# Attention denominators from a ones column of V, spread by a VectorE shuffle, in a one-core block kernel with a written-out order

## The chip, the core and the metric

The kernel runs on one core of a Trainium2 chip. A core has TensorE (PE, which multiplies matrices; PEld is its loading of weights), VectorE (DVE), ScalarE (ACT), GpSimd (POOL), SyncE (SP, which here only starts DMAs) and 16 DMA engines. The metric is the time of one execution in device microseconds. The kernel before took 169.4 us, the median of three runs (169.27, 169.4 and 171.14 us).

## The reference, cut to what matters

One block of a transformer on 2048 tokens of width 448, conditioned by a vector `c`:

```python
sa, ca, ga, sb, cb, gb = (silu(c) @ w_mod) in six rows
h = layernorm(x) * (1 + ca) + sa
q, k, v = h @ wqkv                                  # 16 heads of width 28
idx = pos[:, None] - 2 * arange(8)[None, :]         # 8 keys per query, 2 apart
logits = einsum('bhsd,bhswd->bhsw', q, k[idx]) * 28 ** -0.5
o = einsum('bhsw,bhswd->bhsd', softmax(logits, masked where idx < 0), v[idx])
x = x + ga * (o @ wo)
h = layernorm(x) * (1 + cb) + sb
x = x + gb * (gelu(layernorm(h) @ w1 + b1) @ w2 + b2)
```

## The kernel before

**Tiles.** Keys lie 2 tokens apart, so even and odd tokens never meet; they are two halves (`NS = 2`) of 1024 positions. A *token tile* p (0 to 7) is 128 positions of both halves. Attention goes in nine *batches* i (0 to 8) of 114 query positions, each as two windows (`j`) of 57 queries over 64 keys. The MLP goes in four *MLP tiles* t of two token tiles.

**Stages.** `front_ln` normalizes a token tile on DVE into a `zy` buffer (`stats`, `rstd`, `normalize`, `tail`), turns it on its side (by PE for tiles 0 and 1, by an SP transpose DMA `zT<-zy` for the others) and `affine` makes `hT` of it. `front_qk` makes q and k of tiles 0 and 1; `natural_qk` does so for tiles 2 to 7 (PE into `pq`, a copy into `zy`, transpose DMAs into `qT` and `kT`). `attention(i)` makes V of its windows (`pv`, copied to a `vb` buffer with 32 columns per head, of which 28 are V and 4 are padding), the logits (`lt`), their exponentials (`et`, ACT), the band mask (DVE multiplies `et` by `mask`), then on PE the denominators (`pd`) and the weighted values (`po`). The denominators' reciprocal is made on ACT as exp(-ln) in `den`, and the DVE product `omul` writes `po` times `den` into `qT`, over the queries that are no longer needed.

In `pd`, 8 matmuls per batch multiply a matrix of ones by `et`, so that all 32 rows of a head hold the sum of its weights; for the first window of batch 0 the first seven keys do not exist, and `ones_k` has zeros there:

```python
nc.tensor.matmul(pd.t[HP * r:HP * r + HP, j, 0:2 * SBE], lhsT=ones_k[rows, int(i == j == 0), :],
                 rhs=et.t[rows, r].rearrange("p m c -> p (m c)"), ...)
```

`out_proj(p)` (matmuls `wo{p}` into `pw`) needs the `omul` of the batches that cover tile p: batches 0 and 1 for tile 0, 1 and 2 for tile 1, 2 and 3 for tile 2, 3 and 4 for tile 3. It adds the residual on DVE (named `x1`), makes the second and third layernorm, and ends in a transpose DMA `yT<-zy`. `mlp(t)` multiplies by `w1` (tiles `p`, from `yT`), applies gelu on ACT, multiplies by `w2` and stores. ACT has to load another table between exponentials and gelu, so the work is cut into `PHASES`: batches 0 to 4 and MLP tile 0; batches 5 and 6 and MLP tile 1; batches 7 and 8 and MLP tiles 2 and 3.

**What sets the order.** Every step is a numbered task with the tasks it needs. Nothing is scheduled on the chip: `ORDER` lists the task numbers in the order in which they are written into the engines' queues, each queue runs strictly in that order, and `SLOTS` says which buffer of its kind each tile gets. An entry `84:A` gives the task to ACT (A), DVE (D) or POOL (P) instead of its usual engine; `55+12@55` writes 12 *fillers* ahead of task 55, which are matmuls on zeros into a PSUM tile that is free at that moment. PSUM has four places of two banks for `pq`, `pv`, `lt`, `pd`, `po`, `pw` and the MLP's tiles. ACT's and POOL's table and mask set-up, all DMA starts of SP and the constant fills of DVE are tasks too.

Of the kernel before, what the change touches and what calls it, by code (L numbers as in the profile page):

```python
# [15 lines left out]
KT, KS = 4, 64  # L16
# [33 lines left out]
]  # L50
ORDER = """
3 14 17 0 1 15 5 9 10 18 11 16 13 19 20 2 6 24 21 73 55+12@55 26 12 71 25 56 72 74 57 75 22 58 77 23 59 62 60 27 61 76
4 32 67 66 78 68+11@68 108 63 28 110 64 30 84:A 89:P 69 79 65 31 70 88:P 109 111 80 83 112:P 34 81 87:A 85 29 93:P
90:A 101+9@101 114 113 36 82 94+3@94 91 95 115:D 92:A 102 86 103 116 144 96 120:A 97 99 135 104 106 117:A 98 142 118:A
105 145 119:A 143 133 146 100 121 136 134 148 137 126 107 147 7 149:D 138 127 150 122 139 124 129 198 190 123 140 191
200 141 199 128 269 125 271 236 270 130 207 40 209 33 201 241 210 38 237 208 272 238 273 37 185 242 152 202 35 154 151
153:A 8 278 187 239 203 159 211 204 188 205:D 212 206 155 279 213 186 243 240 214:A 160 156 192 215 307 157 189 275
161 274 158 280 171 308 281 282 193 162 172 244 245 284 195 283 163 217 173 285 246 276:D 219 39 218 167 216 277 247
447 164 196 248 225 286 168 224 165 169:D 174 312 42 309 313 228 166 310 314 220 170 226 311 290 221 289 229 222 288
315 194 287 230 558 232 197 317 176 560 233 318 175 316 177 223 249 319 234 49 227 320 250 231 251 559 321 235 345 253  # L60
342 346 373:R 254 252 324 46 255 343 322 44 257 48 340 561 323 325 256 41 326 258 374 51 482 54 378 344 375 52 379 299
347 47 259 376 43 328 292 327 300 341 260 348 291 329 301 261 330 295 293 262 263 380 350 264 294 131 296 132 304 333
297 303 377 45 351 334 331 381 265 349 332 305 266 335 382 352 267:A 483 383 268 337 336 384 448 338:D 339 385 353 53
# [89 lines left out]
def kernel(  # L153
# [143 lines left out]
    dconst(0.45, consts, ["vpad", "ones"])  # L297
# [664 lines left out]
```

## Time and profile before

| | before |
|---|---|
| median of three runs | 169.4 us |
| the profiled execution | 170.37 us, of which the span of the core is 168.6 us |
| busy: PE, DVE, ACT, POOL | 95%, 67%, 60%, 25% of the span |
| matmul instructions | 2126 |
| DMA | 18.78 MB, nearly all in the first 70 us |
| granted PE clock | full in every slice |

The span runs from the core's first instruction to its last; a profiled execution is one of many, and this one took 0.97 us more than the median of the three timed runs. The trace gives for each group of instructions the busy time, the mean length of one and the idle time of its engine just before it, with what ended that idle time. Instructions of one engine overlap at their ends, so what one more instruction costs is the distance between two starts in the timeline, which is a little less than its length.

### The profile page before, as it was taken

To read this page: it belongs to the slowest core of one execution; us is meant where nothing else is said; L and a number is where in the kernel's file an instruction comes from. 1 tells how busy PE (TensorE), PEld (TensorE's weight loads), DVE (VectorE), ACT (ScalarE), POOL (GpSimd) and SP (SyncE) were. 2 spreads that over 40 slices of the span, in tenths; PEclk is the share of its full clock that TensorE was granted. 3 is DMA by queue.
4 is the path that set the end of the run, shared out by engine and by line. 5 is a ranking of instruction groups with operands and counts; after the bars stand their busy time and mean duration, and the time that the engine had idled before them with its cause. 6 is when DMAs were issued, how large, how long until landed. Compare 5 with 4: busy or idle time off the path is not lost.

```text
span 168.6 us, 4965 instructions
## 1 busy us (share of the span) xinstructions
PE 160.9 (95%) x2126; PEld 84.0 (50%) x2126; DVE 113.2 (67%) x277; ACT 101.3 (60%) x139; POOL 42.0 (25%) x69
## 2 busy tenths in 40 slices
PE   7999969987999999999999999999999999999992
PEld 4778535444554544435565443555544455344562
DVE  7869898758899969897837869465596940400112
ACT  3378888949379946869557167986318440099000
POOL 3235251002030400319300033850003156008100
PEclk9999999999999999999999999999999999999999
DMA  5999989699999799300150000028020006110002
GB/s 158 323 336 291 167 253 172 129 158 255 188 227 287 211 160 201 100 0 0 25 106 2 4 0 2 4 49 188 4 95 14 0 4 120 46 67 0 0 27 82
DMA packets 35573, 18.78 MB, mean 111 GB/s; under 512 B 28507, under 2 KB 34592, under 8 KB 35552
## 3 DMA queue, kind: packets, MB, share of 16 engines
q1 hardware_dynamic: 35548, 18.47, 47.6%
q8 instruction: 16, 0.26, 0.6%
q14 instruction: 5, 0.04, 0.1%
q10 hardware_dynamic: 4, 0.00, 0.0%
HBM read 9.81 MB, written 1.84 MB: 69 GB/s over the span
## 4 chain that ended last, share of the span: by engine, by line
PE 77%; DMA 13%; DVE 4%; issue 2%; POOL 2%; SPq 1%; ACT 1%; POOLq 0%; DVEq 0%
PE p L882 26%; PE p L547 22%; PE pw L802 7%; DMA zT<-zy 7%; PE pq L547 5%; PE p L553 4%; DMA x_all<-in_A_x_dram 4%; PE pv L547 3%; PE po L770 3%; DMA wm_st<-in_w_mod_dram 3%; PE lt L737 2%; DVE hT L501 2%; PE pv L705 2%; PE pd L759 1%; DVE stt L455 1%
## 5 line engine op out<-in xcount | busy, mean ns | idle before, releaser
L863 ACT ACTIVATE hm<-p,b_col 128x512 bf16<-128x512 f32 x56 | 33.6, 695 | 30.6 <-PE p L553 26.1
L882 PE MATMUL p<-w_s,hm 128*128 128x448 bf16 (+1 forms) x238 | 44.5, 342 | 0.0
L547 PE MATMUL p<-yT,w_s 128*128 128x512 bf16 x168 | 38.1, 380 | 0.0
L468 POOL TENSOR_TENSOR rs_all<-mvs,neg_half 128x2 f32<-128x2 f32 x23 | 16.4, 719 | 75.1 <-DVE mvs L457 75.1
L882 PEld LDWEIGHTS <-hm 128*128 128x128 bf16 x238 | 22.6, 98 | 18.9 <-issue 0.6
L547 PEld LDWEIGHTS <-w_s 128*128 128x128 bf16 x168 | 15.8, 98 | 21.0 <-issue 3.2
L888 DVE TENSOR_TENSOR x_all<-p,x1p 128x896 bf16<-128x896 f32 (+2 forms) x10 | 8.8, 899 | 23.7 <-PE p L882 23.7
L744 ACT ACTIVATE et<-lt 128x928 bf16<-128x928 f32 x18 | 16.1, 940 | 6.7 <-PE lt L737 6.6
L455 DVE BATCH_NORM_STATS2 stt<-x_all 128x6 f32<-128x448 bf16 x32 | 18.6, 610 | 1.6 <-DMA x_all<-in_A_x_dram 1.4
L547 PE MATMUL pq<-wqk_st,hT 128*128 128x448 bf16 x72 | 15.0, 353 | 1.8 <-DVE hT L501 1.5
L840 POOL TENSOR_TENSOR x1p<-x_all,gbb_bc 128x448 f32<-128x448 bf16 x16 | 16.5, 1060 | 0.0
L787 DVE TENSOR_TENSOR qT<-po,den 128x912 bf16<-128x912 f32 x9 | 10.0, 1106 | 7.1 <-ACT den L781 6.7
L802 PE MATMUL pw<-wo_s,qT 128*128 128x448 bf16 x64 | 13.1, 353 | 0.0
L750 DVE TENSOR_TENSOR et<-et,mask 128x928 bf16<-128x928 bf16 x18 | 11.0, 640 | 2.2 <-ACT et L744 2.1
L627 ACT CAST zy<-pq 128x896 bf16<-128x896 f32 x11 | 9.7, 911 | 2.7 <-issue 2.0
L809 DVE TENSOR_TENSOR x_all<-pw,x_all 128x896 bf16<-128x896 f32 x8 | 8.7, 1088 | 3.9 <-PE pw L802 3.9
L779 ACT ACTIVATE den<-pd 128x928 f32<-128x928 f32 x9 | 8.5, 952 | 4.7 <-PE pd L759 4.7
L818 DVE TENSOR_TENSOR h<-h,mod_bc 128x896 bf16<-128x896 bf16 x16 | 10.4, 655 | 0.2
L547 PEld LDWEIGHTS <-hT 128*128 128x128 bf16 x72 | 6.5, 98 | 8.1 <-DVE hT L501 2.0
L455 DVE BATCH_NORM_STATS2 stt<-h 128x6 f32<-128x448 bf16 x16 | 9.5, 611 | 0.1
L781 ACT ACTIVATE den<-den,den_bias 128x928 f32<-128x928 f32 x9 | 9.4, 1068 | 0.2
L802 PEld LDWEIGHTS <-qT 128*128 128x128 bf16 x64 | 6.0, 98 | 6.0 <-issue 0.4
(114 smaller groups left out, 177.3 us busy)
## 6 DMA issues: line engine op xcount, KB each, us to landing
w_s<-in_B_w_dram SPq DMA_DIRECT2D x7, 224.0 KB, 3.3
out_dram<-x_all SPq DMA_DIRECT2D x7, 224.0 KB, 2.0
x_all<-in_A_x_dram SPq DMA_DIRECT2D x3, 448.0 KB, 6.5
wmod<-in_w_mod_dram SPq DMA_DIRECT2D x3, 448.0 KB
w_s<-in_B_w_dram SPq DMA_DIRECT2D x3, 448.0 KB, 4.8
wqk_st<-in_A_wqkv_dram SPq DMA_DIRECT2D x3, 225.0 KB, 4.3
wm_st<-in_w_mod_dram SPq DMA_DIRECT2D x1, 672.0 KB, 4.6
x_all<-in_A_x_dram SPq DMA_DIRECT2D x2, 224.0 KB
```

Source lines behind the costliest of these rows:

```text
L455: add("DVE", 0.53, lambda: nc.vector.bn_stats(out=stt[:, w, b, 0:6], in_=src()), reads=reads, bufs=bufs, after=early if w == b == 0 else ( ...
L468: ways = {"POOL": (0.55 + 0.17 * n, lambda: nc.gpsimd.tensor_tensor(out=r, in0=v, in1=neg_half[:, 0:n], op=ALU.pow))}
L547: nc.tensor.matmul(out(), lhsT=lhs(kt, slice(0, 128)), rhs=rhs(kt, slice(0, 128)), start=first and kt == 0, stop=not first and kt == KT - 2)
L627: add("ACT", 0.80, lambda to=to, src=src: nc.scalar.copy(out=to(), in_=src()), bufs=[pq, st], reads=["zpad"], writes=[(st, 0)], name="evac ...
L744: exps.append(add("ACT", 0.83, lambda half=half, lt=lt: nc.scalar.activation(out=et.t[:, 2 * half:2 * half + 2].rearrange("p r m c -> p r ...
L750: nc.vector.tensor_tensor(out=ev, in0=ev, in1=mask[:], op=ALU.mult)
L787: nc.vector.tensor_tensor(out=qT[:, :, LEAD + q00:LEAD + q00 + 2 * WQ], in0=po.t[:, :, 0:NS * 4 * WQ].rearrange("p j (m c) -> p m j c", c=WQ),
L802: nc.tensor.matmul(pw.t[:, s, 0:D], lhsT=qT[:, KT * s + ft, LEAD + 128 * p:LEAD + 128 * p + 128], rhs=wo_s[:, ft, :], start=(ft == 0), sto ...
L818: add("DVE", 0.55, lambda vec=vec, op=op: nc.vector.tensor_tensor(out=h2.t[:], in0=h2.t[:], in1=vec.unsqueeze(1).to_broadcast([128, NS, D] ...
L840: add("POOL", 1.0, lambda n=n: nc.gpsimd.tensor_tensor(out=x1p.t[:, n, :], in0=xn(p, n), in1=gbb2_bc[:], op=ALU.add), reads=[f"x{p}", "gbb ...
L863: gelus.append(add("ACT", 0.585, lambda f=f, a=a, p1=p1s[g]: nc.scalar.activation(out=hm.t[:, f].rearrange("p n c -> p (n c)"), in_=p1.t[: ...
L882: nc.tensor.matmul(p2.t[:, n, 0:c1 - c0], lhsT=hm.t[:, f, n, q * 128:(q + 1) * 128], rhs=w2_s[:, f, c0:c1], start=(f == parts[0][0]), stop ...
```

## The change

The denominators no longer have matmuls of their own. The 29th column of each head in `vb`, padding before, is filled with ones, so that row 28 of each head's 32 rows in `po` holds the sum of the weights. A new DVE instruction, `stream_shuffle`, copies that row to all 32 rows of its head, from `po` in PSUM into `den` in SBUF, as fp32. `Ln` on ACT then works in place on `den` (912 elements per row instead of 928, from SBUF instead of PSUM), followed by the same `Exp` and `omul`. For batch 0 the ones of the first seven keys are set to zero ahead of `po` and set back behind it. `pd` and its PSUM place are gone.

Beside this the reciprocal square root of tile 0's layernorm is split into two tasks, one for each half; a wait between two groups of `front_qk` is relaxed; eight PSUM places without work (`idle`) are added as targets for fillers; and `SLOTS` and `ORDER` are new as a whole (of them the diff shows the first and the last line of `ORDER`).

```diff
@@ SLOTS, ORDER: all lines
-3 14 17 0 1 15 5 9 10 18 11 16 13 19 20 2 6 24 21 73 55+12@55 26 12 71 25 56 72 74 57 75 22 58 77 23 59 62 60 27 61 76
+3 17 14 0 1 15 11 13 7 18 16 19 5 12 6 20 59+6@59 4 10 2 24 8 25 81 21 9 63+7@63 55 82 22 84:P 64 65 23 79 27 66 67 80
...
-680 691 688 689 694 693 701 683 692 682 684 695 685 702 697 703 704 709 698 696 710 699 705 711 700 706 712 707 708
+694 699 720 709 707 721 712 722 710 713 711 723 716 714 717 715 718 719 57+13@57 61+3@61
@@ consts
         for vb in vbufs:
-            nc.vector.memset(vb[:, :, :, DH:HP], 0.0)
-        nc.vector.memset(ones_k[:], 1.0)
-        nc.vector.memset(ones_k[0:WIN - 1, 1, :], 0.0)
+            nc.vector.memset(vb[:, :, :, DH:DH + 1], 1.0)
+            nc.vector.memset(vb[:, :, :, DH + 1:HP], 0.0)
@@ behind c_cols
+    for i in range(8):
+        idle = psum("idle")
+        add("PE", 0.0, lambda: None, reads=["warm_w"], bufs=[idle], fills=[idle], instr=0, name=f"fl{i}")
@@ front_ln
-            rstd(0, 2 * p, 2, on_act)
+            for b, m in ((2 * p, 1), (2 * p + 1, 1)) if p == 0 else ((2 * p, 2),):
+                rstd(0, b, m, on_act)
@@ front_qk
-    after=last_qk[-2:] if small and k else (),
+    after=last_qk[-1 if u[0] == 0 else -2:] if small and k else (),
@@ attention
+        ones = lambda value: nc.vector.memset(vb.t[0:WIN - 1, :, :, DH:DH + 1], value)
+        if i == 0:
+            add("DVE", 0.06, lambda: ones(0.0), reads=["vpad"], bufs=[vb], fills=[vb], name="ones")
...
-        add("PE", 0.25, dmm, reads=[(et, 0), (et, 1), "ones"], bufs=[et, pd], fills=[pd], mode="64x32", instr=16, name=f"pd{i}")
...
+        if i == 0:
+            add("DVE", 0.06, lambda: ones(1.0), bufs=[vb], needs=[P.tasks[-1]], name="ones")
-        den = sb("den", [128, 2, 4 * NS, WE], FP32, "den")
-        add("ACT", 0.87, lambda: nc.scalar.activation(out=flat(), in_=pd.t[:, :, 0:2 * SBE], func=ACT.Ln, scale=DEN_SCALE), ...
+        den = sb("den", [128, 2, 4 * NS, WQ], FP32, "den")
+        add("DVE", 1.0, lambda: nc.vector.stream_shuffle(out=den.t[:].rearrange("p j m c -> p j (m c)"), in_=po.t[:, :, 0:NS * 4 * WQ], mask=[DH] * HP),
+            bufs=[po, den], fills=[den], name="spread_den")
+        add("ACT", 0.87, lambda: nc.scalar.activation(out=den.t[:], in_=den.t[:], func=ACT.Ln, scale=DEN_SCALE), ...
```

What the new order does to the queues is seen at three places. The first is SP's queue of DMA starts right at the program's beginning, behind the loads of tile 0 and of the modulation weights (`x_all` is the input, `wqk_st` and `wqr_st` are the weights of q and k). Before:

```order
L338 DMA x_all<-in_A_x_dram 128x896
L324 DMA wqk_st<-in_A_wqkv_dram 128x900
L328 DMA wqr_st<-in_A_wqkv_dram 64x900 x2
L324 DMA wqk_st<-in_A_wqkv_dram 128x900 x2
L338 DMA x_all<-in_A_x_dram 128x2x896 x2
```

and in the change:

```order
L337 DMA x_all<-in_A_x_dram 128x896
L327 DMA wqr_st<-in_A_wqkv_dram 64x900
L323 DMA wqk_st<-in_A_wqkv_dram 128x900 x3
L337 DMA x_all<-in_A_x_dram 128x2x896
L327 DMA wqr_st<-in_A_wqkv_dram 64x900
```

One of the two `wqr_st` loads has moved behind the load of token tiles 2 and 3 (the first `128x2x896`).

The second place is DVE's queue from the first `omul` (`qT<-po,den`) to the first `x1` (`x_all<-pw,x_all`), in the middle of the first phase. Before:

```order
L688 COPY hw<-hT 128x1024
L787 TENSOR_TENSOR qT<-po,den 128x8x114
L628 CAST zy_98<-pq 128x32x28
L750 TENSOR_TENSOR et<-et,mask 128x928 x2
L501 TENSOR_SCALAR hT<-zT,mod_col 128x2x256 x4
L688 COPY hw<-hT 128x1024
L787 TENSOR_TENSOR qT<-po,den 128x8x114
L652 TENSOR_TENSOR wo_s<-wo_s,mod_bc 128x896 x2
L787 TENSOR_TENSOR qT<-po,den 128x8x114
L809 TENSOR_TENSOR x_all<-pw,x_all 128x896
```

and in the change, from the shuffle of batch 0 on:

```order
L778 STREAM_SHUFFLE den<-po 128x912
L504 TENSOR_SCALAR hT<-zT,mod_col 128x2x256 x2
L757 TENSOR_TENSOR et<-et,mask 128x928 x2
L480 TENSOR_SCALAR zy_98<-x_all,mvs,rs_all 128x448
L788 TENSOR_TENSOR qT<-po,den 128x8x114
L778 STREAM_SHUFFLE den<-po 128x912
L656 TENSOR_TENSOR wo_s<-wo_s,mod_bc 128x896 x2
L504 TENSOR_SCALAR hT<-zT,mod_col 128x2x256
L788 TENSOR_TENSOR qT<-po,den 128x8x114
L504 TENSOR_SCALAR hT<-zT,mod_col 128x2x256
L810 TENSOR_TENSOR x_all<-pw,x_all 128x896
```

Each `omul` has a shuffle ahead of it now; the window copies `hw<-hT` have left DVE's queue (one is on ACT, three are on POOL), and so has a part of the `hT` steps (to ACT).

The third place is DVE's queue where the third layernorms of token tiles 0 and 1 end (`zy<-h`), which their transposes wait for. Before:

```order
L477 TENSOR_SCALAR zy_99<-h_1206,mvs,rs_all 128x448
L787 TENSOR_TENSOR qT<-po,den 128x8x114
L477 TENSOR_SCALAR zy_96<-h_1320,mvs,rs_all 128x448 x2
L490 COPY zy_96<-zy_96 128x2x64
L787 TENSOR_TENSOR qT<-po,den 128x8x114
L809 TENSOR_TENSOR x_all<-pw,x_all 128x896
```

and in the change:

```order
L778 STREAM_SHUFFLE den<-po 128x912
L757 TENSOR_TENSOR et<-et,mask 128x928
L819 TENSOR_TENSOR h_1267<-h_1267,mod_bc 128x896
L480 TENSOR_SCALAR zy_98<-h_1203,mvs,rs_all 128x448
L458 BN_STATS stt<-h_1267 128x6 x2
L460 BN_AGGR mvs<-stt 128x2
L480 TENSOR_SCALAR zy_98<-h_1203,mvs,rs_all 128x448
L674 CAST b_col<-pb_1428 128x14
L460 BN_AGGR mvs<-stt 128x2
L778 STREAM_SHUFFLE den<-po 128x912
L480 TENSOR_SCALAR zy_99<-h_1267,mvs,rs_all 128x448 x2
L788 TENSOR_TENSOR qT<-po,den 128x8x114 x2
```

The shuffles of batches 3 and 4 stand ahead of these layernorms now, both `omul` behind them, and the small copy `zy<-zy` has gone to POOL.

More of the change, by code (lines that the diff above doesn't have):

```diff
@@ L56 @@
[L56 to L60, printed above, removed]
@@ L227 @@
     rs_all = cst.tile([128, 3, 2 * NP], FP32, name="rs_all")
-    ones_k = cst.tile([128, 2, HP], BF16, name="ones_k")
     den_bias = cst.tile([128, 1], FP32, name="den_bias")
@@ L598, in front_qk @@
                 last_qk.extend(summed([item(k, a) for a in range(2)], NS * n / 2400 + 0.0025,
-                                      ([] if first else [f"W{half}{k}" for k in range(KT - 1)] + [f"h{kt}_{p}" for kt in range(KT - 1) for p in u] + rk), [pqs[k]], [pqs[k]], after=last_qk[-2:] if small and k else (),
+                                      ([] if first else [f"W{half}{k}" for k in range(KT - 1)] + [f"h{kt}_{p}" for kt in range(KT - 1) for p in u] + rk), [pqs[k]], [pqs[k]], after=last_qk[-1 if u[0] == 0 else -2:] if small and k else (),
                                       name=f"qk{u[0]}_{half}" + "ab"[k], split=rk if first else None))
@@ L752, in attention @@
             add("DVE", 0.56, msk, port=True, bufs=[et], reads=["mask"], writes=[(et, half)], name="mask")
-        pd, po = psum("pd"), psum("po")
-        def dmm():
-            for j in range(2):
-                rows = slice(WK * j, WK * j + WK)
-                for r in range(4):
-                    nc.tensor.matmul(pd.t[HP * r:HP * r + HP, j, 0:2 * SBE], lhsT=ones_k[rows, int(i == j == 0), :],
-                                     rhs=et.t[rows, r].rearrange("p m c -> p (m c)"),
-                                     start=True, stop=True, tile_position=(WK * j, HP * r))
+        po = psum("po")
         def pmm():
@@ L788, in omul @@
                                     in0=po.t[:, :, 0:NS * 4 * WQ].rearrange("p j (m c) -> p m j c", c=WQ),
-                                    in1=den.t[:, :, :, 0:WQ].rearrange("p j m c -> p m j c"), op=ALU.mult)
+                                    in1=den.t[:].rearrange("p j m c -> p m j c"), op=ALU.mult)
         add("DVE", 1.02, omul, bufs=[po, den], writes=[f"o{i}", f"qj{i - 1}"], name="omul")
```

44 lines of the change are left out of this document (26 added, 18 removed), and 15 rows, old and new, of tables (ORDER, SLOTS).

## The prediction

> **What bounds the kernel now.** I read the page's first lines, then the busy time by stage, then what PE waits for, then the timelines of the engines that it waits for.
>
> ```profile
> span 168.6 us, 4965 instructions
> PE 160.9 (95%) x2126; PEld 84.0 (50%) x2126; DVE 113.2 (67%) x277; ACT 101.3 (60%) x139; POOL 42.0 (25%) x69
> ```
>
> The stages, cut where PE takes up tile 2's q and k (22.97), at the first `x1` on DVE (44.21), at the first MLP matmul (64.78) and at PE's end (165.65); the columns are length, then busy us of PE, PEld, DVE, ACT, POOL:
>
> ```profile
> 0.00:22.97 22.97, 20.02 (x311) 14.02 (x312) 18.84 (x79) 15.04 (x25) 8.78 (x27) 1.00 0.90 256
> 22.97:44.21 21.24, 19.47 (x388) 9.99 (x389) 16.53 (x36) 16.48 (x20) 2.60 (x4) 1.00 1.04 187
> 44.21:64.78 20.57, 20.57 (x385) 10.40 (x383) 18.93 (x43) 14.90 (x18) 3.15 (x4) 1.00 0.94 217
> 64.78:165.65 100.87, 100.86 (x1047) 49.55 (x1046) 58.51 (x120) 54.85 (x78) 27.44 (x35) 1.00 0.18 41
> 165.65:168.60 2.95, 0.00 (x0) 0.00 (x0) 0.39 (x1) 0.00 (x0) 0.00 (x0) 1.00 0.36 117
> ```
>
> From 44.21 on PE never stops, so a change there pays only as much as it takes off PE, and costs what it makes PE wait. Before, PE stands still three times for other engines:
>
> ```profile
> PE pq L547 <- DVE hT L501: 1.5, 1, 1.5
> PE pd L759 <- ACT zy L627: 1.3, 1, 1.3
> PE pq L547 <- DVE zy L628: 0.3, 1, 0.3
> ```
>
> The first ends stage one (1.47 us); the others belong to the 21.24 - 19.47 = 1.77 us of stage two. So 3.24 us of waits, and PE work, are all that can be won. DVE is the other thing to see: busy 78% in stage two and 92% in stage three, before a single shuffle is added.
>
> **What leaves PE.** The first and the last `pd` groups, of eight that hold the nine batches, and the dearest; each cost is the distance to the next row's start:
>
> ```profile
> 28.11 0.73 PE L759 MATMUL pd<-et,ones_k 64*32 64x464 bf16 x16
> 28.53 0.88 PE L770 MATMUL po<-et,vb 64*32 64x57 bf16 x64
> 86.87 0.39 PE L759 MATMUL pd<-et,ones_k 64*32 64x464 bf16 x8
> 87.19 2.82 PE L882 MATMUL p<-w_s,hm 128*128 128x448 bf16 x14
> 115.69 0.39 PE L759 MATMUL pd<-et,ones_k 64*32 64x464 bf16 x8
> 115.90 0.73 PE L770 MATMUL po<-et,vb 64*32 64x57 bf16 x64
> ```
>
> The groups cost 0.42 (two batches), 0.19, 0.33, 0.20, 0.21, 0.32, 0.21 and 0.21: 2.1 us in all, though the 72 matmuls are 364 ns long each, because eight run side by side. 0.6 lies in stage two, 0.5 in stage three, 0.95 in stage four.
>
> **What comes to DVE.** Nine shuffles of 912 fp32 elements from PSUM to SBUF, which no row shows. The nearest rows, all one pass over PSUM of the same length, and the fastest copy of that length:
>
> ```profile
> L787 DVE TENSOR_TENSOR qT<-po,den 128x912 bf16<-128x912 f32 x9 | 10.0, 1106 | 7.1 <-ACT den L781 6.7
> L628 DVE CAST zy<-pq 128x896 bf16<-128x896 f32 x1 | 1.1, 1080 | 0.0
> L723 DVE CAST vb<-pv 128x896 bf16<-128x896 f32 x1 | 1.0, 1049 | 0.0
> L688 DVE COPY hw<-hT 128x1024 bf16<-128x1024 bf16 x4 | 1.7, 427 | 0.1
> ```
>
> I take 1.05 us; 0.43 is the end below, and twice a pass, 2.1, the end above (if moving between rows needs a second one). The Trainium skill, page "VectorE: DVE Perf Modes", section "The perf-mode tier table", gives the shuffle one element per cycle in every case, about 2400 ns for 2048 elements; worked out from it, an estimate is 1.2 us, and the sum below would be 0.15 x 5 = 0.75 us higher. No run here shows it.
>
> On ACT, `Ln` now reads SBUF, as `Exp` does: 1068 instead of 952 ns, 0.1 us more per batch.
>
> ```profile
> L779 ACT ACTIVATE den<-pd 128x928 f32<-128x928 f32 x9 | 8.5, 952 | 4.7 <-PE pd L759 4.7
> L781 ACT ACTIVATE den<-den,den_bias 128x928 f32<-128x928 f32 x9 | 9.4, 1068 | 0.2
> ```
>
> The chain from `po` to `omul` is thus shuffle, `Ln`, `Exp`, `omul` = 1.05 + 1.07 + 1.07 + 1.1 = 4.3 us, where before `Ln` could start beside `po` and the rest took about 3.
>
> **Stage one: 0.9 us less.** The wait that ends it comes from the chain of tiles 2 and 3: their load, statistics, normalization, transpose, `hT`.
>
> ```profile
> 6.33 6.03 DMA x_all<-in_A_x_dram
> ...
> 15.91 0.07 POOL mask L279
> ...
> 17.21 0.29 POOL zy L489
> ...
> 17.61 3.41 DMA zT<-zy
> ```
>
> One `wqr_st` load (112.5 KB; 0.45 us at the 256 GB/s of this stage) is no longer ahead of the load. The mask set-up, 1.3 us of POOL's queue between 15.91 and the tail copy at 17.21, is moved to the program's start. The normalization of tile 3 is late next and gives back most of it: I take 0.5 of the 1.3 (bounds 0 and 1.3). On PE the new order writes 31 fillers ahead of the modulation's matmuls, where 23 stood:
>
> ```profile
> 1.25 2.74 PE L381 MATMUL ps_c<-warm_w 128*128 128x256 bf16 x12 [1.25 <-DVE warm_w L241]
> 8.26 1.14 PE L381 MATMUL pq<-warm_w 128*128 128x256 bf16 x9
> ```
>
> Eight more at 0.11 to 0.22 us are 0.9 to 1.8 us. What hides them is the 1.47 us wait behind; as that shrinks by 0.9, up to 1.2 us could come through. I count nothing, as fewer fillers stand behind.
>
> **Stage two: 0.5 us less.** PE loses 0.6 us of `pd`. DVE gets three shuffles (3.2 us) and loses two window copies, three `hT` steps and two small copies (about 2.1 us). The steps that stand around them:
>
> ```profile
> L455 DVE BATCH_NORM_STATS2 stt<-x_all 128x6 f32<-128x448 bf16 x32 | 18.6, 610 | 1.6 <-DMA x_all<-in_A_x_dram 1.4
> L477 DVE TENSOR_SCALAR zy<-x_all,mvs,rs_all 128x448 bf16<-128x448 bf16 x16 | 5.9, 398 | 1.4 <-POOL rs_all L468 0.8 <-ACT rs_all L466 0.3
> L501 DVE TENSOR_SCALAR hT<-zT,mod_col 128x512 bf16<-128x512 bf16 x11 | 4.7, 477 | 2.9 <-DMA zT<-zy 2.9
> L750 DVE TENSOR_TENSOR et<-et,mask 128x928 bf16<-128x928 bf16 x18 | 11.0, 640 | 2.2 <-ACT et L744 2.1
> ```
>
> From start to start each is some 50 ns less. Walking PE and DVE along their new queues with these I find two waits. First, `po` of a batch stands right behind tile 2's 16 matmuls (22.1 + 3.0 = 25.1), but DVE has, from the landing of tile 3 at 20.6 (21.02 before; the rest of the 0.9 comes from one of the four `hT` steps going to ACT), still 3 `hT`, 2 statistics, 3 normalizations, 3 masks and 0.5 of small steps to do: 1.3 + 1.1 + 1.1 + 1.7 + 0.5, until 26.2: 1.1 us. Second, tile 4's q and k wait for `hT` steps that now stand behind a shuffle and an `omul`: 0.8 us. That is 1.9 for the 1.77 before. So the first `x1`, 44.21 before, starts at 44.2 - 0.9 - 0.5 = 42.8.
>
> **Stage three: 0.3 us lost.** Here DVE bounds. PE cannot enter the MLP ahead of `yT` of tiles 0 and 1, nor ahead of `wo2` and `wo3`, which need the `omul` of batches 3 and 4.
>
> ```profile
> 44.21 1.09 DVE L809 TENSOR_TENSOR x_all<-pw,x_all 128x896 bf16<-128x896 f32 x1 [0.43 <-PE pw L802]
> 58.37 1.11 DVE L787 TENSOR_TENSOR qT<-po,den 128x912 bf16<-128x912 f32 x1
> 60.13 0.20 DVE L490 COPY zy<-zy 128x128 bf16<-128x128 bf16 x1
> 58.97 2.90 SPq L833 DMA_TRANSPOSE yT<-zy  x2
> ```
>
> ```profile
> yT<-zy SPq DMA_TRANSPOSE x8, 3.8
> ```
>
> Before, DVE needs 60.13 - 44.21 = 15.9 us for the rows between, nearly without a gap. After, one `omul` (1.03) and one window copy (0.34) are gone from between and two shuffles (2.1) and a memset (0.06) are in: 16.7. From 42.8 that ends at 59.5; POOL's tail copy ends near 59.9, and `yT` lands 3.8 us later, 63.7 (before: second issue at about 60.42, landing 64.2). The two `omul` follow at 59.5 and 60.6, and between them `wo2` and `wo3` (1.55 us each) run until 63.7. So the MLP starts at 63.7 instead of 64.78: 1.1 us won so far, of 2.6 that PE's queue alone would have given (`pd` 1.1 and the first wait).
>
> **Stage four: 0.95 us less**, the four `pd`. PE's other work is the same. The longer chain is covered: behind the last `po` of batches 5 and 6 PE still has 14 and 6 `w2` matmuls, 6 of `pv` and `wo4` (about 6.7 us) ahead of `wo5`, which needs up to 6.2 (batch 6's shuffle waits behind batch 5's and a residual add); behind that of batch 8, 20 `w2` and `wo6` (5.4 us) against 4.3. Without that cover each such place costs its excess, at most 1.5 us. DVE has room: it is busy 58% here. The 16 fillers behind the last matmul (9 took 0.97 us above, so 1.7) lie beside the last result and store, the 2.95 us behind 165.65.
>
> **Sum:** -0.9 - 0.5 + 0.3 - 0.95 = -2.05, rounded to -2.1. On the profiled execution's span that is 166.5; this execution's 170.37 us lies 0.97 above the median, so I take it from the median: 169.4 - 2.1 = **167.3 us**.
>
> **Rivals.**
> 1. *PE bounds throughout.* If masks, `hT` and `yT` always come in time, PE loses 2.1 us of `pd` and 3.24 of waits: 164.1. For it: an order searched as a whole, and 4.7 us of DVE idle time in stage two. Against it: stage three's 92%. Chance 0.18.
> 2. *The cover is gone early.* The fillers come through (up to 1.2), or the walk misses a wait, and the MLP starts at 64.8 as before or a little later; only stage four pays, or that too goes to the longer chain: 168.4 to 169.8. For it: five shuffles lie ahead of the MLP on its fullest engine. Chance 0.22.
> 3. *The shuffle makes it slower.* All five shuffles ahead of the MLP lie on the path, three ahead of `x1` and two behind. At 2.1 us each adds 1.05: 167.3 + 5.2 = 172.5. It decides from 1.05 + 2.1 / 5 = 1.47 us a shuffle. For it: the length is not in the trace. Against it: every one-pass PSUM row stands at 1.05 to 1.1. Chance 0.07.
>
> **How the numbers follow.** The forecast, 166.0 to 168.3, has 0.53. The range, 164.6 to 169.7, takes in most of rivals 1 and 2 and leaves out about 2 in 10: rival 1's lower half, rival 3 and the ends of the rest. Two per cent, about what a measurement of this kernel can tell from no change, is 166.0 below and 172.8 above: faster has rival 1 and the forecast's lower edge, 0.28; slower has the upper half of rival 3, 0.04; within 2%, 0.68.
>
> **What would show it.** The shuffle at 1.0 to 1.2 us; PE's first tile 2 matmul near 22.1; waits of PE on masks and on `hT` together near 1.9 us up to `x1` at 42.8; the first MLP matmul near 63.7 with PE waiting on `omul` or `yT` just before; from there to PE's last matmul about 99.9 us; ACT's `Ln` near 1.07. I am wrong if PE arrives at the MLP without a wait (rival 1), if it waits at `wo` in stage four, or if shuffles are over 1.4 us.

## The result: 0.5% slower, 3.4 us above the forecast

| | before | after |
|---|---|---|
| median, runs taken in turn on one chip | 169.82 us (20 runs) | 170.68 us (20 runs) |
| after / before | | 1.0054, 95% interval 1.0029 to 1.0079 |
| the profiled execution, its span | 170.37, 168.6 us | 171.29, 169.5 us |

The forecast was 167.3 us, range 164.6 to 169.7. Of the 3.4 us by which 170.68 lies above it, 0.4 is the base (the 20 runs of before have a median of 169.82, not 169.4) and 3.0 is the change itself, +0.9 instead of -2.1. Both profiled executions lie 0.6 us above their medians, so their difference (0.92) may be read for that of the medians (0.86).

The page of after, its first two lines:

```profile
span 169.5 us, 4900 instructions
...
PE 162.2 (96%) x2079; PEld 85.5 (50%) x2079; DVE 121.4 (72%) x284; ACT 106.0 (63%) x149; POOL 47.5 (28%) x76
```

Its stages, cut as before at tile 2's q and k, the first `x1`, the first MLP matmul and PE's end (length, then busy us of PE, PEld, DVE, ACT, POOL):

```profile
0.00:23.39 23.39, 20.29 (x320) 14.92 (x321) 18.75 (x78) 14.50 (x27) 9.82 (x28) 1.00 0.90 250
23.39:43.93 20.54, 19.39 (x369) 9.61 (x369) 16.57 (x35) 18.63 (x26) 1.95 (x3) 1.00 0.97 167
43.93:66.48 22.55, 20.79 (x361) 10.06 (x360) 21.72 (x48) 16.34 (x20) 7.95 (x10) 1.00 1.04 206
66.48:166.46 99.98, 99.97 (x1016) 49.58 (x1017) 63.91 (x126) 56.54 (x80) 27.77 (x35) 1.00 0.19 47
166.46:169.50 3.04, 1.75 (x17) 1.32 (x14) 0.39 (x1) 0.00 (x0) 0.00 (x0) 1.00 0.18 57
```

Against before: +0.42, -0.70, +1.98, -0.89 and +0.09, together +0.9. Stages two and four came out as forecast; stage one was to lose 0.9 and grew, stage three was to grow by 0.3 and grew by 2. What PE waits for where stage three and stage one end:

```profile
PE p L551 <- DMA yT<-zy: 1.4, 1, 1.4
...
PE pq L557 <- ACT vb L724: 0.8, 1, 0.8
```

and the two transposes in the chain that ended last (start of the issue, us to landing):

```profile
16.96 4.69 DMA zT<-zy
...
61.13 5.22 DMA yT<-zy
```

In before the first of these was issued at 17.61 and took 3.41 us, the second was issued at 60.35 and took 3.38. So `zT` of tile 3 is issued 0.65 us earlier, but takes 1.3 us longer and lands at 21.65 instead of 21.02; the second `yT` is issued 0.8 us later and takes 1.8 us longer.

**One execution is not the kernel.** To see what repeats, both kernels were run once more for a second trace:

> The kernel before, a second time, for its profile: single executions of it lie between 168.3 and 171.5 us (and one at 173.5), so a stage that differs between two executions of one kernel by as much as between the two kernels explains nothing. The table of the first: tile 2 begins at 22.97, the first x1 21.24 later, the MLP 20.57 after that, PE ends 100.87 after that. If each stage repeats within 0.3 us, the differences of the change stand; if stage one moves by 1 us, only the other stages do.

> The changed kernel a second time, for its profile. First: tile 2 at 23.39, then 20.54, 22.55 and 99.98. In two other executions with the same order there (the runs with wmod moved and with wide fillers) yT of tiles 0 and 1 took 5.4 to 5.5 and 4.3 to 4.5 us, not 6.28 and 5.22, so I expect stage three at 21.6 to 22.1, with PE's wait for yT at 0.4 to 0.7 instead of 1.40, and tile 2 between 23.2 and 24.2.

They took 169.38 and 173.11 us. Stage one and three of the second trace of before, then of after:

```profile
0.00:21.96 21.96, 19.14 (x312) 13.61 (x312) 18.06 (x79) 14.30 (x24) 7.88 (x26) 1.00 0.89 258
...
43.26:63.82 20.56, 20.56 (x384) 10.40 (x383) 18.91 (x43) 14.89 (x18) 3.15 (x4) 1.00 0.91 214
```

```profile
0.00:26.11 26.11, 21.62 (x321) 15.44 (x322) 19.31 (x78) 14.40 (x27) 9.76 (x28) 0.93 0.83 223
...
46.60:68.27 21.67, 20.71 (x362) 9.95 (x361) 20.93 (x47) 16.23 (x20) 7.97 (x10) 1.00 0.99 215
```

Stages two to four repeat within 0.1 us, but for stage three of after, where `yT` takes 6.28 and 5.22 us in the first trace and 5.5 and 4.2 in the second. Stage one varies by 1 us and more in both. The 26.11 is an extreme: PE waited four times there between 6.6 and 11.1 us, 2.5 us in all, and the granted clock was 0.50 from 11.0 to 14.4 us. Over the traces of this work with the order of before there, tile 2 begins at 22.97, 21.96 and 21.64; with the order of after, or nearly so, at 23.39, 26.11, 23.19, 23.81, 24.03 and 24.23. So stage one is mostly 1.5 to 2 us longer, and from tile 2 to PE's end after takes 143.07 and 142.15 us where before takes 142.67 and 142.72. I read this as the 0.9 us being lost in stage one, with stage three keeping the other stages from winning it back; two traces each, of executions that lie up to 2.4 us from their median, do not show it.

### The profile page after: what moved, and what is told of

Its sections match the earlier page's. It is cut to its first block, busy times and chain, and to the rows that moved or that the text cites. A ratio compares the mean times of both kernels' runs of the same rounds, so it can differ in the third digit from the quotient of the medians.

```text
span 169.5 us, 4900 instructions
## 1 busy us (share of the span) xinstructions
PE 162.2 (96%) x2079; PEld 85.5 (50%) x2079; DVE 121.4 (72%) x284; ACT 106.0 (63%) x149; POOL 47.5 (28%) x76
## 4 chain that ended last, share of the span: by engine, by line
PE 71%; DMA 10%; DVE 9%; ACT 4%; issue 4%; POOL 1%; DVEq 0%; POOLq 0%
PE p L883 25%; PE p L551 22%; DMA zT<-zy 6%; PE pw L803 5%; PE p L557 4%; PE pq L551 4%; DMA yT<-zy 3%; PE lt L744 3%; PE po L769 2%; DVE zy L480 2%; DVE stt L458 2%; DMA x_all<-in_A_x_dram 2%; PE pv L551 1%; DVE et L757 1%; PE pq L557 1%
## 5 line engine op out<-in xcount | busy, mean ns | idle before, releaser
L471 POOL TENSOR_TENSOR rs_all<-mvs,neg_half 128x2 f32<-128x2 f32 (+1 forms) x22 | 17.3, 787 | 54.1 <-DVE mvs L460 53.5
L841 POOL TENSOR_TENSOR x1p<-x_all,gbb_bc 128x448 f32<-128x448 bf16 x16 | 17.1, 1096 | 0.0
L780 ACT ACTIVATE den<-den 128x912 f32<-128x912 f32 x9 | 8.7, 964 | 6.7 <-DVE den L778 6.7
L778 DVE STREAM_SHUFFLE den<-po 128x912 f32<-128x912 f32 x9 | 10.6, 1180 | 0.0
L492 POOL COPY zy<-zy 128x128 bf16<-128x128 bf16 x8 | 2.7, 334 | 25.3 <-DVE zy L480 21.6
L782 ACT ACTIVATE den<-den,den_bias 128x912 f32<-128x912 f32 x9 | 9.5, 1058 | 0.2
```

The costliest lines, as they stand in the source:

```text
L471: ways = {"POOL": (0.55 + 0.17 * n, lambda: nc.gpsimd.tensor_tensor(out=r, in0=v, in1=neg_half[:, 0:n], op=ALU.pow))}
L778: add("DVE", 1.0, lambda: nc.vector.stream_shuffle(out=den.t[:].rearrange("p j m c -> p j (m c)"), in_=po.t[:, :, 0:NS * 4 * WQ], mask=[DH ...
L841: add("POOL", 1.0, lambda n=n: nc.gpsimd.tensor_tensor(out=x1p.t[:, n, :], in0=xn(p, n), in1=gbb2_bc[:], op=ALU.add), reads=[f"x{p}", "gbb ...
```

## Experiments

All stand against the kernel before, run in turn on the same chip. Theory A: loads put beside the transposes make these land late. Theory B: the shuffles on DVE are the price. Theory C: a transfer of PE instructions that runs in a transpose's flight holds it. Theory D: the transpose is slow for another reason (the one ahead of it, the loads behind it). In the table "tile 2" is the instant at which PE takes up tile 2's q and k in the trace, and the next three columns are the lengths of stages two, three and four; `zT` is that of tile 3, `yT` those of tiles 0 and 1, as us from issue to landing.

| kernel | median | ratio, 95% interval | tile 2 | to x1 | to MLP | to PE's end | zT | yT |
|---|---|---|---|---|---|---|---|---|
| before | 169.82 | | 22.97 | 21.24 | 20.57 | 100.87 | 3.41 | 3.59, 3.38 |
| after | 170.68 | 1.0054, 1.0029 to 1.0079 | 23.39 | 20.54 | 22.55 | 99.98 | 4.69 | 6.28, 5.22 |
| three w2 loads behind yT | 170.96 | 1.0067, 1.0035 to 1.0099 | 23.19 | 20.17 | 21.02 | 101.38 | 4.71 | 3.08, 3.40 |
| five w2 loads, in order of use | 170.36 | 1.0043, 1.0013 to 1.0073 | 24.23 | 20.32 | 20.91 | 100.41 | 4.69 | 3.38, 3.13 |
| wmod behind zT of tile 4 | 174.58 | 1.0258, 1.0222 to 1.0293 | 23.81 | 22.91 | 22.13 | 99.99 | 4.88 | 5.51, 4.45 |
| stage one's order | 170.32 | 1.0046, 1.0016 to 1.0076 | 22.56 | 20.81 | 21.41 | 99.94 | 4.48 | 5.27, 4.11 |
| V's copy first | 170.37 | 1.0043, 1.0019 to 1.0068 | 22.73 | 20.84 | 21.98 | 100.00 | 4.30 | 5.78, 4.12 |
| wqr early | 170.93 | 1.0071, 1.0035 to 1.0107 | 23.84 | 20.24 | 22.05 | 99.99 | 4.86 | 5.56, 4.49 |
| no shuffles | 170.96 | 1.0052, 1.0020 to 1.0085 | 24.03 | 20.85 | 21.45 | 99.90 | 4.64 | 5.69, 4.86 |
| shuffles in the old order | 184.08 | 1.0821, 1.0755 to 1.0888 | 21.64 | 27.72 | 25.64 | 103.35 | 3.17 | 3.06, 3.56 |
| 18 fillers wide | 172.21 | 1.0148, 1.0090 to 1.0206 | 24.23 | 21.50 | 21.57 | 100.00 | 5.04 | 5.41, 4.33 |
| five edits | 170.04 | 1.0001, 0.9974 to 1.0028 | 23.36 | 21.05 | 20.82 | 100.27 | 4.76 | 3.13, 3.23 |
| all edits | 169.87 | 0.9999, 0.9965 to 1.0034 | 22.65 | 20.91 | 20.88 | 100.63 | 3.21 | 4.44, 3.19 |

**Are the shuffles the price?** The changed kernel without them:

```diff
-        add("DVE", 1.0, lambda: nc.vector.stream_shuffle(out=den.t..., in_=po.t..., mask=[DH] * HP), ...)
-        add("ACT", 0.87, lambda: nc.scalar.activation(out=den.t[:], in_=den.t[:], func=ACT.Ln, scale=DEN_SCALE), ...)
+        add("ACT", 0.87, lambda: nc.scalar.activation(out=den.t..., in_=po.t[:, :, 0:NS * 4 * WQ], func=ACT.Exp, scale=DEN_SCALE), ...)
```

> The changed kernel without its nine shuffles: the step that stood as Ln on ACT reads the weighted values straight from PSUM (as an exponential with a tiny scale, of the same length), so the division is by a meaningless number and the denominators are left out. DVE has 9 x 1.07 us less, five of them ahead of the MLP; order, loads and transposes are the same. If DVE with its shuffles bounds stages two and three, tile 2 to MLP (43.1 us in the changed kernel) shrinks by 2 us or more and the time to 168.5 or less; if loads ahead of transposes and PE's own queue bound them, it shrinks by under 1 us, 170 or more.

170.96 us, ratio 1.0052 where after has 1.0054: nothing is saved that can be told. Its page and its stages two and three:

```profile
PE 161.9 (96%) x2079; PEld 85.2 (50%) x2079; DVE 112.1 (66%) x266; ACT 105.8 (63%) x149; POOL 48.3 (29%) x76
```

```profile
24.03:44.88 20.85, 19.17 (x369) 9.46 (x369) 13.41 (x30) 19.30 (x27) 1.96 (x3) 1.00 1.05 181
44.88:66.33 21.45, 20.80 (x361) 10.00 (x360) 18.94 (x43) 15.43 (x19) 8.00 (x10) 1.00 1.02 211
```

DVE has 9.3 us less to do, and PE's stages are about as long as in the second trace of after (20.49, 21.67). So theory B falls for stages two and three of the new order as it stands. `yT` lands as late there as in after (5.69 and 4.86 us), and no run leaves out the shuffles with the loads ahead of `yT` moved, so what the shuffles cost then is open. In the old order the mechanism is dear:

```diff
 the kernel before without pd; where Ln stood on ACT:
+            nc.vector.stream_shuffle(out=den.t..., in_=po.t[:, :, 0:NS * 4 * WQ], mask=[DH] * HP)
+            nc.scalar.activation(out=den.t[:], in_=den.t[:], func=ACT.Ln, scale=DEN_SCALE)
```

> The mechanism alone in the old order: the kernel before without the matmuls pd, the ones in V's 29th column, and a shuffle on DVE where Ln stood on ACT (for batches 0, 2 and 3 Ln and Exp are moved behind the weighted values, on which they now depend). PE loses 2.1 us; DVE gains nine shuffles of 1.05 us, five of them ahead of the MLP, and the queue is not searched anew. If the shuffles' time on DVE is the price of the change, the stages up to the MLP grow by up to 5.3 - 1.1 = 4.2 us and stage four shrinks by up to 0.95: 170 to 173. If it is hidden beside other work, 168 to 169. The difference to the changed kernel is what the new order is worth.

184.08 us, a miss for every expectation; stages two to four:

```profile
21.64:49.36 27.72, 20.59 (x370) 9.75 (x362) 20.62 (x45) 17.72 (x21) 3.47 (x5) 0.94 0.95 172
49.36:75.00 25.64, 21.88 (x367) 10.73 (x368) 21.20 (x48) 15.21 (x18) 3.15 (x4) 0.93 0.69 167
75.00:178.35 103.35, 100.53 (x1015) 48.91 (x1014) 62.87 (x128) 54.95 (x78) 27.43 (x35) 1.00 0.17 37
```

PE stands still 7.1, 3.8 and 2.8 us in them, and part of the time the granted clock was lower (0.94 and 0.93). Its two longest waits are not for DVE:

```profile
PE pv L545 <- ACT zy L625: 3.6, 1, 3.6
...
PE pv L551 <- ACT zy L625: 2.8, 1, 2.8
```

These copies of q and k into `zy` stand behind `Ln` and `Exp` in ACT's queue, and `Ln` waits for the shuffle, 19.2 us in eight waits. DVE itself is busy 20.6 of 27.7 us in stage two. So in the old order a large part of the price is that the longer chain from `po` to `omul` holds up ACT's queue; theory B, the time on DVE, is not shown there either. The new order is worth 13.4 us to the mechanism (184.08 against 170.68). Where does it give part of that back?

**The loads beside `yT`.** SP's queue around it, before and then after:

```profile
56.66 0.57 SPq L369 DMA_DIRECT2D w_s<-in_B_w_dram  x1
58.97 2.90 SPq L833 DMA_TRANSPOSE yT<-zy  x2
```

```profile
57.23 1.63 SPq L373 DMA_DIRECT2D w_s<-in_B_w_dram  x3
59.20 4.42 SPq L834 DMA_TRANSPOSE yT<-zy  x2
```

Three loads (672 KB) go ahead of it instead of one (448 KB), and they go later. Moved behind it:

```diff
 ORDER (279 and 350 are yT of tiles 0 and 1; 53, 50, 54 are loads of w2)
-... 53 361 342 50 140 ... 343 54 276 ... 279 ... 350 395 ... 313 ... 48 461 365 49
+... 361 342 140 ... 343 276 ... 279 ... 350 53 50 54 395 ... 313 ... 48 461 365 49
```

> The changed kernel with three loads of w2 (3 x 224 KB), which stand on SP right ahead of the transposes yT of tiles 0 and 1, moved right behind them. Theory A (the new order puts loads ahead of the transposes that PE waits for): yT is issued near 58 and 60.5 and lands about 3.5 us after its issue, as in the kernel before (3.59 and 3.38), instead of 6.28 and 5.22; PE enters the MLP when its own queue is done, near 65.1 instead of 66.48, and the kernel takes about 1.3 us less than the changed kernel, 169.3. Theory B (the shuffles on DVE make stage three long; the landing is late because its data is late): the MLP begins no earlier than 66.2 and the time stays within 0.3 us of 170.7.

Theory A holds up to the MLP: `yT` lands 3.08 and 3.40 us after its issue, PE enters the MLP without a wait at 64.37. But the time is 170.96, no less. The next stage gives it back, in the queue of DVE and then of PE:

```profile
64.37:165.75 101.38, 100.34 (x1017) 49.45 (x1016) 66.07 (x127) 54.87 (x78) 28.96 (x35) 1.00 0.24 53
```

```profile
69.44 0.62 DVE L664 TENSOR_TENSOR w_s<-w_s,mod_bc 128x896 bf16<-128x896 bf16 x1 [1.51 <-DMA w_s<-in_B_w_dram]
```

```profile
84.81 0.86 PE L769 MATMUL po<-et,vb 64*32 64x57 bf16 x64 [0.51 <-DVE et L757]
86.01 0.66 PE L769 MATMUL po<-et,vb 64*32 64x57 bf16 x62 [0.35 <-DVE et L757]
```

The first `w2` part now lands at 69.4, DVE waits for it, and the masks of batches 5 and 6 behind it come after PE. With all five late loads behind `yT` in the order in which DVE takes them up:

```diff
-... 279 ... 350 395 ...
+... 279 ... 350 48 50 53 49 54 395 ...
```

> The changed kernel with all five late loads of w2 behind yT of tile 1, in the order in which DVE's scaling steps take them up (parts 0, 2, 5, 1, 6) and ahead of kT of tile 7. With the three loads moved alone, the MLP began at 64.37, but DVE then waited 1.51 us at 69.44 for part 0 of w2 and PE 0.9 us for masks behind it. If that was the price, part 0 now lands near 65.1, DVE has no such wait, and the 2.1 us at the MLP's start stay until the end: PE's stage four 100.0 us long and about 1.3 to 1.8 us less than the changed kernel, 169.1. If DVE bounds the part behind the MLP's start in any case (its steps from the first x1 on and the shuffles), masks again come after PE and the time stays near 170.7.

Stage three 20.91, stage four 100.41, 170.36 us: 0.3 less than after, of 1.3 to 1.8 expected, and the intervals (1.0013 to 1.0073 and 1.0029 to 1.0079) do not tell this from nothing. This trace's tile 2 begins 0.8 us later than that of after, and the wait for `yT` that is removed was 1.40 us in the first trace of after but 0.6 in the second.

**Stage one.** Three runs with one edit each, and one with two:

```diff
 wmod behind zT of tile 4 (217); 180 are the matmuls that need it, 318 is V of batch 2
-210 36 212 ... 213 34 194:R ... 214 35 ... 217 ... 180 258 38 202 318:R
+210 212 ... 213 194:R ... 214 ... 217 36 34 35 ... 258 38 202 318:R 180
 V's copy (195) ahead of the hT step that waits for zT (162:A)
-161 162:A 222 163 215 195
+161 195 162:A 222 163 215
 stage one's order: that move, and on DVE the copies of w_mod and mod_col early
-69 74 31 85 29 87 70 117 ... 75 119 ... 118 28 120 96 72 121 ... 77 78 122 100:P 89 90
+69 74 31 70 75 85 29 87 117 ... 119 ... 28 72 ... 77 78 89 90 118 120 121 92 96 122 100:P
 wqr early (26, ahead of the load 27 of tiles 2 and 3)
-8 25 81 21 ... 23 79 27 66 67 80 86 68 26
+8 25 26 81 21 ... 23 79 27 66 67 80 86 68
```

> The changed kernel with the three wmod loads (224 + 448 + 448 KB), which stand right behind the transpose zT of tile 3, moved behind that of tile 4, and the modulation matmuls that need them moved behind V of batch 2. Theory A (loads issued while a transpose is under way slow it): zT of tile 3 lands near 20.4 (latency 3.4 as before) instead of 21.66 (4.69), PE starts on tile 2 near 22.6 instead of 23.39 and the time falls by up to 0.8 us, to about 170; a wait at the modulation matmuls near 30 may take some back. Theory B: latency stays at 4.5 or more, since queues are served in order and nothing behind a transpose matters to it; time within 0.3 us of 170.7.

A miss for theory A in this place: with no load behind it but two of 98 KB, `zT` still takes 4.88 us. The loads come too late and cost 4 us. (With the three `w2` loads and stage one's order besides, 174.03.)

> The three edits together. Theory A: they add up, tile 2 near 22.3, MLP near 64.2, stage four 100.0 as measured: about 2.2 us less than the changed kernel, 168.5, and faster than the kernel before by about 1.3 us. Theory B (DVE with its shuffles is the bound up to the MLP): tile 2 starts earlier but the MLP starts no earlier than 65.5, time 170 or more.

> The changed kernel with the second wqr load back ahead of the loads of tiles 2 and 3, its place before the change. If that load is the cause (it lands at 12.2 to 12.9 and PE waits 0.85 us for POOL's Wqr copy at 13.4 in two of the executions), tile 2 begins about 0.8 us earlier than its middle of 24.0 and the time falls to 169.9. If the transpose zT of tile 3 sets the end, tile 2 begins no earlier, or up to 0.45 later since the load of tiles 2 and 3 is put back by as much, and the time is 170.7 to 171.1.

170.93: not that load either, though PE waits 0.85 us for it in some executions.

> The changed kernel with one move alone: on ACT the copy of V of batch 0 ahead of the hT step that waits for zT of tiles 2 and 3. PE then no longer waits for that copy (0.8 to 1.1 us in every execution of the changed order) but for the hT steps, which end 0.6 us earlier. Tile 2 0.5 us earlier, 170.2; 170.7 if another wait follows at once.

> The changed kernel with two changes of order in stage one and no DMA moved: on DVE mod_col stands ahead of the aggregates and the Wqr copy of the start (its inputs' copies ahead of tile 0's second normalization), and on ACT the copy of V of batch 0 stands ahead of the hT step of tiles 2 and 3 that waits for zT. If PE's queue of stage one is late because mod_col is (9.42 at its end against 8.48 before), q and k of tile 0 start near 9.8 instead of 10.29 and PE stands ready for tile 2 near 22.1; if the transpose alone sets the end, PE then waits for hT until 22.8, 0.6 us earlier than 23.39. Time 170.1 if this carries through to the end, 170.7 if yT's landing at the MLP absorbs it, since yT then lands where it did.

170.37 and 170.32. V's copy on ACT stood behind a step that waits for `zT`, though its own data was there and PE needed the place it frees; with it first, tile 2 begins at 22.73 and 22.56, and the medians are 0.3 us lower, which the intervals do not tell from nothing. In the run with this move alone PE waits for nothing at tile 2: there its own queue, and not `zT`, ends the stage. The early `mod_col` adds nothing that can be told.

**Why `zT` is late.** In the flight of most transposes that take long, the trace shows a transfer of 16 KB of PE instructions on a DMA queue of its own. Fewer PE instructions ahead move these transfers back:

```diff
-        for _ in range(n):
-            nc.tensor.matmul(t.sums[0].t[:, 0, 0:256], ..., rhs=warm_w[:, 0:256], ...)
+        w = 512 if n == 18 else 256
+        for _ in range(n * 256 // w):
+            nc.tensor.matmul(t.sums[0].t[:, 0, 0:w], ..., rhs=warm_w[:, 0:w], ...)
 in the second: w = 512 if n > 3; in the third, the kernel before: w = 128 if n == 11
 in the last: range(0 if n in (6, 7, 10, 18) else n), all 256 wide
```

> The changed kernel with the 18 fillers ahead of the modulation's matmuls made 9 of double width (512 columns instead of 256): the same PE time, but 18 PE instructions fewer, so that every later 16 KB transfer of PE instructions starts some 18 instructions later (about 0.8 us where PE works on V, near 19 us). Theory C (a transpose that is under way when such a transfer runs lands 1.3 us late): the transfer at 19.07 us moves to about 19.9, zT of tile 3 is done first and lands near 20.3 (latency 3.4) instead of 21.66 (4.69), PE starts on tile 2 near 22.6 instead of 23.39; the transfer at 40.14 also moves out of the flight of zT of tile 7 (latency about 3.6 instead of 5.0). Time about 0.5 us less, 170.2, if no other transpose is hit instead. Theory D (the second of two transposes takes 4.7 us because of the first): its latency stays near 4.7 and the time at 170.7.

> The changed kernel with nearly all start fillers of double width and half the number: 40 PE instructions fewer ahead of stage one's work at the same PE time. The 18 of the earlier run moved the second instruction transfer from 19.1 to 20.4 us, still within zT's flight (17.45 to 22.49); 40 should move it to about 21.5. Theory C (a transfer in its flight holds the transpose): zT of tile 3 lands 3.3 us after its issue, near 20.8, tile 2 begins near 22.8 and zT of tile 7 lands 1.3 us earlier too; time 169.5. Theory D (the pair of transposes takes so long anyway, or the loads behind hold it): latency stays above 4.2 and time at 170.7.

> The kernel before with its 11 fillers ahead of the modulation's matmuls made 22 of half the width (128 columns): about the same PE time, 22 PE instructions more, so that the instruction transfer at 20.23 us comes about 0.8 us earlier. Theory C: it then runs in the flight of zT of tile 3, as in the changed kernel, which lands near 22.3 instead of 21.02; PE starts on tile 2 near 24.2 instead of 22.97, and the kernel takes up to 1.2 us longer, 171. Theory D: landing at 21.0 and time at 169.8, unless the narrow fillers take longer than the wide ones.

> The changed kernel without the 41 fillers ahead of the first products of PE (those that write into the idle places and ahead of the first q and k). PE has nothing to do there otherwise, so its real work begins no later; 82 PE instructions fewer move the second instruction transfer some 3 us later, near 22 us, behind the landing of zT of tile 3. Theory C (the transfer in its flight holds the transpose): zT of tile 3 lands 3.3 us after its issue, tile 2 begins near 22.9 and the time falls to 169.8 or less. Theory D (its own pair or the loads behind hold it): 4.3 us or more, time 170.7. Should the granted clock of PE fall without the fillers, stage one grows and the profile's clock row shows it: 171 or more.

The first moved the transfer from 19.07 to 20.37, which is 2.9 us behind the issue: of the 16 completions that the trace records for `zT`, 15 came within 3.38 us and the last at 5.04, where in after all 16 came between 4.54 and 4.69. The time rose to 172.21 for a reason told below. In the second (170.13) the transfer began 2.8 us behind the issue, and again only the last completion was late (5.01). In the third (170.39) the transfer came later (21.05), not earlier as I expected: 3.7 us behind the issue, and yet `zT` took 4.29. That is a long flight which theory C does not explain. In the last (172.15) no transfer ran in the flight. The profiled executions of the second and the last took 174.46 and 174.63 us, far above their medians, so they tell of these transposes, but not of what the time of the kernel depends on. DMAs while `zT` is in flight (q8 is the queue of PE's instructions; rows of a queue with packets, MB and share, and of an issue with us to landing), after and then without fillers, where no row of q8 stands:

```profile
q8 instruction: 1, 0.02, 1.2%
...
zT<-zy SPq DMA_TRANSPOSE x1, 4.7
```

```profile
q1 hardware_dynamic: 1630, 0.47, 77.1%
...
zT<-zy SPq DMA_TRANSPOSE x1, 3.1
```

No instruction transfer, 3.1 us. The 19 traces hold 266 `zT` and `yT`. Behind 70 us, where little else is loaded, 83 of them had no such transfer beginning 1 to 3.1 us after their issue; they took 3.20 us (median), and none more than 4.01. Of the 31 that had one, 19 took 4.20 to 4.97 us, and 12 took 3.03 to 3.08; in these 12 the transfer began 2.44 us after the issue or later. Ahead of 70 us, 58 with such a transfer took 4.76 us (median; 6 of them under 3.5) and 94 without it 3.62, many of these behind loads. In the kernel before such a transfer starts 2.6 us behind the issue of `zT` and does not delay it (3.41), and with all edits 2.5 us behind (3.21). So theory C is likely for `zT`, but not shown: no run moved only the transfer, and the third run above does not fit it. For the first `yT` the loads are enough: in the second trace of after, with stage one's order and with V's copy first, no such transfer begins 1 to 3.1 us behind its issue, and it takes 5.52, 5.27 and 5.78 us.

**Together.** The five edits (`mod_col`, V's copy, the `w2` loads, `b_col` ahead of a normalization, one mask of batch 5 ahead of one that waits for POOL), and the same with wide fillers and the early `wqr`:

> The changed kernel with the order edits that helped, and two more: mod_col earlier on DVE, V of batch 0 copied ahead of the waiting hT step on ACT, the five late w2 loads behind yT, the small copy b_col ahead of a normalization (PE waits 0.35 us for it at 58), and the first mask of batch 5 ahead of a normalization that waits for POOL (PE waits 0.35 us at 86). From the parts: tile 2 at 22.6, x1 20.4 later, MLP 20.7 after that at 63.7, stage four 100.0: 3 us less than the changed kernel's profile, 168.3 as the profiled time, and 168.5 to 169 as the median, faster than the kernel before by about 1 us. If another wait takes their place, 169.5 or more.

> The five edits of the earlier run (170.04, level with the kernel before) together with the wqr load early and the wide fillers. If zT of tile 3 comes 1.3 us earlier and PE's queue of stage one is no longer held by Wqr, tile 2 begins near 22.0, and with 20.5, 20.8, 100.2 and 4.8 behind PE's end the time is 168.3, faster than the kernel before by 1.5 us. If the transpose stays late: 170.

170.04 and 169.87, where 168.3 to 169 was expected: level with the kernel before, faster than it in neither. The stages of the latter:

```profile
0.00:22.65 22.65, 20.77 (x299) 12.25 (x301) 18.88 (x78) 14.37 (x28) 9.92 (x28) 1.00 0.86 247
22.65:43.56 20.91, 19.37 (x378) 9.71 (x370) 16.65 (x36) 18.84 (x26) 1.96 (x3) 1.00 1.07 175
43.56:64.44 20.88, 20.76 (x361) 9.97 (x360) 20.12 (x46) 16.52 (x20) 7.95 (x10) 1.00 0.82 187
64.44:165.07 100.63, 100.09 (x1015) 49.38 (x1015) 66.93 (x127) 56.39 (x79) 28.65 (x35) 1.00 0.25 54
```

In this trace `zT` lands at 20.87 and PE waits for nothing at tile 2, which still begins only at 22.65: PE's own queue ends stage one. 0.65 us of what the MLP's earlier start wins is lost again in stage four (99.98 in after), where DVE is busy 66.9 us; in before it was 58.5 and in after 63.9, and four shuffles at 1.07 us are 4.3 of the 5.4 between these two.

## Why the prediction was wrong, step by step

- **The shuffle**: 1.05 us taken, start to start 1.07, length 1180 ns. Right. In proportion to the elements, the 2400 ns for 2048 of the Trainium skill, page "VectorE: DVE Perf Modes", section "The perf-mode tier table", give an estimate of 1.07 us and not the 1.2 that the prediction worked out; the trace agrees with the 1.07 from start to start, and with the 1.2 only for the length. `Ln` from SBUF takes 964 ns, not 1068: a tenth too dear.

```profile
L778 DVE STREAM_SHUFFLE den<-po 128x912 f32<-128x912 f32 x9 | 10.6, 1180 | 0.0
```

```profile
L780 ACT ACTIVATE den<-den 128x912 f32<-128x912 f32 x9 | 8.7, 964 | 6.7 <-DVE den L778 6.7
```

- **Stage one, -0.9**: tile 2 begins at 23.39 instead of 22.1, wrong by 1.3 in this trace and by more in the second. The step that failed is "the landing of tile 3 at 20.6": it took the issue forward by the load and by POOL, which was right (16.96 against 17.61), and the latency of before for granted. That latency rose from 3.41 to 4.69, and tile 3 landed at 21.65. It reached PE by a way that I had not walked: the `hT` step given to ACT, which I counted as a gain, held V's copy behind it, and PE waited 0.84 us for that copy. A second step failed beside it, "I count nothing": I let the fillers be hidden and did not walk DVE's new queue to `mod_col`, whose last step moved from 8.31

```profile
8.31 0.17 DVE L424 TENSOR_TENSOR mod_col<-ps_col,mod_col 128x8 f32<-128x8 f32 x1
```

  to 9.25, so that PE's own queue was done only at 22.55 instead of 21.5:

```profile
9.25 0.17 DVE L427 TENSOR_TENSOR mod_col<-ps_col,mod_col 128x8 f32<-128x8 f32 x1
```

  So 0.84 of the 1.3 us is the wait and 0.5 is PE's own queue. The runs show that mending the first is not enough: with V's copy first tile 2 begins at 22.73, and with `zT` in time as well at 22.65, both without a wait. Why `zT` takes 1.3 us longer stays open, with the instruction transfer as the likely cause.
- **Stage two, 20.7**: 20.54. Right, as a length.
- **Stage three, 20.9**: 22.55 and 21.67. DVE's part was right: from `x1` to the end of the last normalization 16.8 us for 16.7 taken. What failed is the term "`yT` lands 3.8 us later": it landed 5.22 us after its issue, since the three loads that the new order puts ahead of it were not priced. With them behind it, it takes 3.1 to 3.4 us (4.44 once) and the stage is 21.02, 20.91, 20.82 and 20.88 us long, as forecast.
- **Stage four, 99.9**: 99.98, and no wait at `wo`. Right, but perhaps by luck: the MLP's late start left DVE time. "DVE has room" is not so in the stage's first 20 us; where the loads are moved and the MLP starts earlier, masks are late and 0.3 to 1.4 us is lost.
- **The rivals**: the shuffle as the bound (from 1.47 us) did not come, nor PE throughout. The second, "the cover is gone early", is nearest, since a walk that missed a wait and an MLP no earlier than before are in it; but it ended at 169.8, and it named neither the loads ahead of `yT` nor V's copy behind `zT`. No rival ended slower than before by a transfer.

## What to carry to other kernels

When an order is new, the latency of a transfer on the path is no constant to be taken from the old trace: price what is queued ahead of it, and look for other DMAs that will run in its flight. A wait removed at one place is worth only what the next engine has spare; here 1.5 us won ahead of the MLP were given back 20 us later where the moved loads came late (1.4 us), and 0.3 to 0.65 us in the other runs. A mechanism and the order that carries it are judged apart: the ones column with its shuffle cost 14 us in the old order and 0.9 in the new one.

## What the chip showed that I had not expected

**A wait of 2 us on PE cost nearly twice itself.** In the run with 18 wide fillers PE waits 1.99 us, and the 12 matmuls behind take 4.07 us (2.44 in after, behind a wait of 0.84), at a granted clock of 0.66:

```profile
24.23 0.36 PE L558 MATMUL pq<-wqr_st,hT 64*128 64x448 bf16 x2 [1.99 <-ACT vb L725]
24.53 4.07 PE L552 MATMUL pq<-wqk_st,hT 128*128 128x448 bf16 x12
```

```profile
25.00:30.00 5.00, 5.00 (x80) 2.11 (x79) 2.74 (x9) 3.85 (x7) 1.67 (x2) 0.66 0.80 146
```

The drop lasts 3.4 us, from 25.2 to 28.6, at 0.50. Such a drop also followed waits of 1.77 us (nearly all start fillers wide, 25.6 to 29.1) and 2.03 us (no fillers at the start, 69.7 to 73.1). Waits of 1.47 (before) and 1.40 us (after) were followed by none: the first six MLP matmuls behind the latter take 1.46 us, as they do without a wait where the loads are moved. The length of one wait does not decide alone, as in the second trace of after the drop came at 11.0, in the last of four waits of 0.74, 0.41, 0.27 and 1.12 us. The Trainium skill, page "TensorE: Matmul & The Clock Gate", section "HAM oscillation — how this bites in real kernels", asks for no gap of PE above some 3.4 us; here 1.77 was enough. So a further half microsecond of delay at this place may cost two; the wait with its drop is also where I put the 1.5 us that this run lost against after, which no run shows.

**The fillers at the start are worth their place.** Without them (172.15 us, ratio 1.0085, 1.0050 to 1.0121) the first q and k matmuls take 0.25 us each, where in after eight take 1.03. No granted clock is on record for these matmuls: the record of this trace begins at 15.07 us, that of before at 6.0, and that of after is empty, so a 1.00 in a row ahead of it is not a reading.

```profile
10.00 2.50 PE L565 MATMUL pq<-hT,Wqk 128*128 128x256 bf16 x10 [1.02 <-ACT hT L506]
```

```profile
10.88 1.03 PE L565 MATMUL pq<-hT,Wqk 128*128 128x256 bf16 x8 [0.21 <-DVE hT L504]
```
